# Windowed attention on one core: VectorE's passes over score tiles split by bank, four shared banks, and TensorE's order as strings

## The chip, the cores and the metric

The kernel runs on one core of a Trainium2 chip. The metric is device time in microseconds for one execution; lower is better. The engines of the core run in parallel and meet at semaphores: TensorE (matmuls, called PE in the profile), ScalarE (ACT), VectorE (DVE), GpSimd (POOL) and SyncE (SP, which here only issues DMAs). Matmul results land in PSUM, eight banks of 512 float32 columns on 128 partitions. Each engine takes its own instructions strictly in the order in which the program lists them.

## What is computed

Cross-shaped window attention on a 224 x 224 image with 96 channels. The first 48 channels attend within horizontal stripes of 8 rows, the other 48 within vertical stripes of 8 columns; each stripe has 1792 tokens. Cut to what matters:

```python
qkv = jnp.einsum('bhwc,cd->bhwd', x, wqkv)
q, k, v = qkv[..., :C], qkv[..., C:2*C], qkv[..., 2*C:]
# horizontal stripes, channels :C2, 28 windows of 8*W tokens
ah = softmax(einsum('bqc,bkc->bqk', qh, kh) * scale)
oh = einsum('bqk,bkc->bqc', ah, vh)
# vertical stripes, channels C2:, the same with windows of H*8 tokens
...
o = pad(oh) + pad(ov)
return jnp.einsum('bhwc,cd->bhwd', o, wo)
```

The shape that decides everything is the score matrix: 56 windows of 1792 x 1792 values, each of which needs an exponential.

## The kernel before, in words

**Tiles.** Windows are handled in pairs (28 pairs, index `P`; 0 to 13 horizontal, 14 to 27 vertical). For one pair, queries are cut into chunks `c` of 512, 512, 512 and 256 columns, keys into 14 blocks of 128. A score tile holds one key block against one query chunk for both windows of the pair: 128 x 1024, two PSUM banks, one bank for each window (for the last chunk two key blocks go together). A pair has 49 such tiles, 1372 in all.

**Two ways to the exponential.** A tile of kind A is scored by four matmuls into banks 0 and 1 or 2 and 3 (`qk_fn`, line 720), and ScalarE takes the exponential into one of 24 `PT` buffers (line 943). A tile of kind P or R is taken off ScalarE and goes through a polynomial on VectorE and GpSimd. TensorE scores it twice, through `s_fn` (line 733): once for the first pass and once more for the last. For kind P, VectorE makes `qb` from the low 16 bits of the scores ("p1", line 1224), GpSimd squares, adds and multiplies (lines 1151 to 1153), and VectorE adds the result onto the second scoring ("f", line 1248). For kind R, VectorE makes two passes over the first scoring (p1 and "p2", line 1237), GpSimd does one square (line 1150), then f follows. `KINDS` says which tiles of a pair are taken off, by chunk; `HOW[P][7]` picks one entry for each pair. Before, 20 pairs have 7 tiles off (all P), 7 pairs have 8 (seven P and one R), and the last pair has 5: 201 in all, 194 P and 7 R.

**Weighted sum and the rest.** `pv_fn` (line 746) multiplies a finished tile by V and adds into one bank for the chunk; VectorE copies the sum out ("ot", line 1206). Other small work fills in ("fills"): transposes of x (505), K, Q and V (522, 569) and the final projection (605, 641), each with a chain of evictions on VectorE (511, 527, 538, 576, 612 and 620, 648 and 653). DMAs of inputs and outputs are issued on SP's queue where a chain of VectorE ends.

**Banks.** Banks 0 to 3 belong to kind A. Banks 4 to 7 are the ring. Before, the chunk's sum takes bank 4 or 5, fills take any free bank of the ring, and the P and R tiles always take 6 and 7 (`PB0 = 6`, keys `PBK`), so that one such tile occupies the two until VectorE has read all 1024 columns.

**Order.** The program is made once, in Python. A planner (`step_pe`, `step_dve`, `step_pool`) steps a modelled time with durations from lines 30 to 36 and decides what each engine does next, by the thresholds in `HOW`. `Sched.commit` records each instruction with the semaphore values that it has to wait for, from `Sched.deps`. Buffers are known to it by keys: ("bank", 6), ("q", 2) for a `qb` buffer, ("PT", 5) for a `PT` buffer. Where an instruction touches a key that another one wrote, it waits for that one; only TensorE's dependences on itself are left out:

```python
for k in reads:
    for (s, _), v in self.wr.get(k, {}).items():
        if not (s == eng and eng == "pe"):
            d.add((s, v))
```

After that, `MERGE` gives the final order of kinds of work on TensorE and VectorE as strings ("q" score, "v" weighted sum, "p" a P or R tile, "f" and "o" fills, "s" a warm-up matmul), and `Sched.merge` reorders the lists accordingly.

Of the kernel before, what the change touches and what calls it, by code (L numbers as in the profile page):

```python
# [20 lines left out]

KINDS = ["PP PP PP ", "PPP PP PP ", "PPP PPP PP ", "PP PP P ", "PPR PP PP ", "PPR PR PP ", "PPR PPR PP ", "PPP PPR PP ", "PPR PPR PR ",
         "RPP RP PP ", "RPP RPP PP ", "PPP PRP PP ", "PPR PP PR ", "PPP PPP  ", "PPR PPP  ", "PPP PP  ", "PPP P  ",
         "PPPP PPP  ", "PPPP PP  ", "PPPP PPPR  "]
# [11 lines left out]
D_P1, D_SQ, D_AF, D_ML = 1.135, 1.9, 1.03, 2.08  # L36


HWIN, HLOW, COLD = 3.4, 0.56, 8.0
# [4 lines left out]

HOW = [
# [7 lines left out]
]  # L55

MERGE = {
    "pe": [
        "ssssssssssssssffffffffffsfsssqqqsfqsffqsfqpqfqpqfqpfqvvvfqqfvvvvqpfvqqpqfvqpqfvqpqfvqpqfvqpqfvqvfqffvqvvqopqvvvqvvqpfqvvqffqqfvqpf",
        "qvvqpvqvvqvvqpoqvvvqpqvfvqvvqpoqvvqvpqvvoqvvqpvqvfqvpqovqvvqpvoqvvqpvqvvfqpvqfqfqfpqvvqfqvvqpvqvvqpvqvoqfvfqvfqvvqpfqvvqvvqvfqvfqo",  # L60
        "oqvvqfvqpvqfqvpqvvqfvqpvqvfqpvqfvvqpfqvoqvvqpvqvvqvpqfvqvvqpoqvvqvpqvvvqfqpvqvvoqpvqfqvpqfqvvqvpoqvvqvvqffqvvqvfqpvqfvvqvpqfqvfqvo",
        "qfoqvvqvfqvpqfvqvpqvfqvvqpvqvvqfpqvvqvvqfvqpvqvfqpoqvvvqvpqfqvvqfqoovqfqvpqfvqvpqvfqvvvqpvqvfqvvqopqvvqvpqvfvqvpqfqfvqvfqfqfvqvpqv",
        "fqvvqvpqovqvvqpvqvvqvfqpvqvvqopqvvoqvvqpvqvfqvpqfqvpqvvoqvvqpvqfqpvqvvqvpoqvvqvvqpvqfqpvqfqvvqvfoqvvqpvqfvqffqvvqfpqvvqvfqfqfoqvvq",
        "pvqvvqopvqvvqvpqfvqvvqvvqfpqvvqvfqvpqfvvqvfqpvqvoqvpqvvqfqvpoqvvqvvqvpqfqvvvqopqvvvqvpqfqvvqpoqvvvqpvqfvqvfqfvqfvqfpqvoqvoqfqfqvvq",
        "fpqvvqvpqvfqvpqfvqvvqvvqpfqvvqpvoqvvqvvqfpqvvqvopqvvqvvqpfqvvqpoqvvvqpvqfqvpqfqvvqfqvopqvvqvfqvfqfvqfvvqvfqpvqfvqfqffqvqpfqvvqpvoq",
        "vvqpvqfvqvvvqopqvvqvvqpvoqvvqpvqvfvqvpqfqvvqopqvvvvqfoqfqvfqpqvvfvqfqffvqvvvqpqfvqpvqvoqvpqvvqfvqfqfpqvvqvpqvqvfqvvqpvqvvfqpvqfvqp",
        "vqvoqvpqvfvqvvqvvqpvqvoqvvqpvqvvoqpvqvvqpvqfqpvqvoqfoqfqfqvvqfpqvvvqvfqffqvvqfpqvoqvvvqpqvfvqpvqvvqpvqvfqpvqfqvvqpfqvvqfvqpvoqvvqp",
        "vqvfqvfqfvqpoqvvqvvqpvvqvoqpvqvfqvvqpvqfqfqvoqvvvvqopqvvvqvpqvfqvfqvfqpvqvvqpvqvvfqvpqovqvvqpvqfqffqffqvpqfvqvvqvqpvqfvqvpoqvqvvpq",
        "vvqvoqvpqvvvqfqpvqvvfqpqvvvvqpoqvvqvvpqfqvpqvvqfqfoqvoqvfvqvfqpvqfvqvpqfvqvvqopqvvqvfqpvqvfqfvqfqpvqfvqvvvqpfqvvqpvqvoqvvvqpoqvvvq",
        "pvqvfqvvqfpqvvvqopqvvqvvqpfqvvqfqpvqfqpvqfqvvfqooqvvqfvqvvfqpqvvvqfpqvfqvvqpvqvoqvpqvfvqvpqfqvvqpvqvvvqpvqfqvvqvpqvvqfvvqopqvvqvvv",  # L70
        "qopqvvvqffqvoqvvqpvqvvfqvvqopqvvvqpvqfvvqpvqfqpvqvvqopqvvvqvpqfqvoqvfqvqvfqpvqfvqfvqfpqvfqvvqfqfvqfoqvvvqpoqvvvqpvqfvqpqvvqfvvqpqv",
        "vvqfvqovqpvqfvqvpqfvqpqfvqvpqfvvqpqvvfqvqvvfqpvqovqvvqpoqvvvqpvqfqvvqpvqovqffqfqvpqfvqpqfvqvpqvvqpqfvqvpqvfvqvpqovqvvvqpoqvvvqvpqv",
        "vqvvqpoqvvqvvqvopqvvqvpqvfqvpqvfqvvqfvqvpqfvqvvqopqvvqfvqpvqvfqvpqfvqvpqfqvpqfvqvpqvfqvvqfpqvoqvvqvpqvvqvpqvoqvpqvvqvvqfvpqvoqvvqp",
        "vqvvqvpqvfqvvoqvqpqvvqvvqofqfvqovqvqpvqvqvfqpvqfqvfqvpqfqvqpfqvvqpvqvfqpvqvfvqpvqfvqvpqvvqovqvpqvoqvvvqpvqvvqfvqpvqvvqpvoqvvqvvqvo",
        "qvqpvqvoqvpqvvoqvvqpvqvfqpqvfvqpqsfqvvqpvvqvqvvfqvpqfvqvfqpqfvqvpqfqvpqfvqvvqpvqfvqvpqvvqovqvpqvvoqvpqvvqfqvvqfpqvvoqvpqvvqvvqfqpv",
        "qfqpoqvvqvpqvvqvqopqvvqvpqvvoqvvqpqvvvqpvqvfqpvqvfqpvqvvqfqvfqffqvvqfvqpfqvvqfvqpvqvqopvqvvqvoqvpqvvqvvqpvqvvqopqvvvqvpqvqvfvqpvqo",
        "vqpqvvqvvqvfqpvqfvqpqvvqopqvvvqvvqpfqvqofvqfqfvqvvqpvqvvqvfqfqpoqvvvqvpqvqvoqpvqvvqvvqpvqfqpfqvvqpfqvvqoqvpqvvqvvfqpoqvvqvvqpvqfvq",
        "vpoqvqvpqvvqvqvvqpqfvqpqvvqfpqvvoqvvqpvqvvqpqvfqpfqvvvqfqffvqoqvvpqvvvqfqvpqvvoqvpqvvqvvqpfqvvqfvqvpqvvoqvoqfvqvvoqvvqpqvfqvpqvfqv",
        "pqvfqvpqvqovqpvqvvvqvfqpvqvfqpvqvfqvfqfqpvqvvqvvfqpqfvqvpqvvqfqpvfqvvqpoqvvqvpqvvvqvqvvoqpvqvvvqpvqvqvfvqvpqvfqvvqpvqfvqpvqfvqpfqv",
        "fqvpqvvqvpqfvqpqvfqoqovqvvqfvqvvqopvqvvqvpqvvqfvqpoqvvqpvqvfqvpqvvqovqvpqvvqoqpvqvqvvqpvoqvvqpqoqvvqvpqvvfqvvqovqvvqpvqovqvvqpvqfv",  # L80
        "qvpqfqvpqfvqvvfqvqpqfqpvqfvqffqfqvpqfvqvvqpfqvvvqpoqvvqpvqvvqovqpvqvvqvvqfpqvoqvvvqpvqvvqoqvvqpvqvqpvoqvvqvvqpvoqvvqpvqvvqvvqvvqfv",
        "qvfqpvqfvqpvqvfqpfqvqpfqvvqpvqvfqooqvvqfvvqqpvfqpqfvqpqvvqvpqvfqvvqpvqvfqvpqvvvqvooqqfvqvvvqoqvpqvvqovqpvqvfvqpvqfvqvpqvvqfvqpvqvv",
        "qpfqvvqpvqvfqvpqfqvpqvvqfqpoqvvqvvqpoqvvqvvqvpqfqvpqvvqfvqvfqvfoqvvqpvqvvqvfqvvqopvqvqvvqovqpvqfvqvpqvvoqvvqpqvvqvpqvfqvpqvfvqvpqf",
        "qfvqvpqfvqvpqvvqfqpoqvvqvvqpvqvvqofqfvqvvqfpqvqvpqvvqfpqvvoqvvqovqvvqvvqfvqpvqvfqpqfvqpvqfvqvopqvvqvvqpvqfqpoqvvvqvvqpfqvvqfqvvqpf",
        "qvvqpvqvvqffqvpqfvqvvqovqvpqvoqvpqvvqvpqvvqfvqpqovqvpqvvqvvvqoqvpqvvqvpqvvqvopqvvqvvqvvqosvqooqvvqvoqvvqvpoqvvqvpqvvqvvqvvvqvvqvvq",
        "voooqvvvqvoqvvvqqooooqsqvvvvvvvoossssss",
    ],
    "dve": [
        "cccccccccccccccccfffffffffffpfpfpfffpffpfpfpfpfpftfffopopffffpfptpoopfpootpoopftpoopoopfpfffpftppooffffpftfoooofpfpfpfpftfppootpfp",
        "oopfpoopftpfopfoffpftfpfoofoofpfpfptpffptfpoopffoooofpfpftpfpoopffpfffftpfpoopfptoopoopftpfpoopfpopotpfpffoopffffptfffoopopopftfpf",  # L90
# [11 lines left out]
    ],  # L102
}
MRG, LATE, BLATE = 0.01, 0.1, 0.05


def kind_of(eng, tag):

# [3 lines left out]
    if eng == "dve":  # L112
        return {"p1": "p", "p2": "p", "f": "p", "ot": "t"}.get(k, "c" if not tag else "o" if tag[2] == "fin" else "f")
# [1235 lines left out]
```

## Time and profile before

| what | us |
|---|---|
| median of 3 runs (1097.43, 1095.25, 1097.43) | 1097.43 |
| span of the profiled execution, first to last instruction (its own device time is not listed apart from the runs) | 1094.3 |
| ScalarE's exponentials: first start 9.37, end of the last 1089.23 | 1171 of them |
| TensorE busy / VectorE busy / GpSimd busy | 1046.6 / 926.5 / 995.2 |
| TensorE's granted clock, mean share | 0.999 |

A busy time is the time in which at least one instruction of the engine was under way. The rows of the profile name a line of the code, an engine, an operation, what it writes and reads, its shape and how often it ran; behind the bar stand the busy time of the group, the mean duration of one in nanoseconds, and the time that the engine had been idle just before, with what ended that wait. Successive instructions of VectorE can overlap: the next may start before the one ahead has ended.

### The profile page before, as it was taken

The numbers are of one execution on the slowest core, as the hardware profiler recorded it, in microseconds if no ns is written. First come the engines' busy times: TensorE is split into PE (matmuls) and PEld (weight loads), VectorE is DVE, ScalarE is ACT, GpSimd is POOL, SyncE is SP. The second block draws the span as 40 slices with busy tenths as digits, with TensorE's granted clock in tenths as the row PEclk, the third lists the DMA queues.
The fourth block names the chain that finished last, engine by engine and source line by source line (L and its number), as shares of the span: only waits on it lengthen the run. The fifth ranks groups of instructions, "written<-read, shape, count | busy, mean of one in ns | idle before, by whom it ended". The sixth has DMA issues, their size and how long they took to land. (4 is left out here: it accounts for less than half of the span.)

```text
span 1094.3 us, 35438 instructions
## 1 busy us (share of the span) xinstructions
PE 1046.6 (96%) x14848; PEld 425.3 (39%) x14848; DVE 926.5 (85%) x1699; ACT 1082.6 (99%) x1182; POOL 995.2 (91%) x626
## 2 busy tenths in 40 slices
PE   8999999999999999999999999999999999999997
PEld 4334344444434444444333333333433333333333
DVE  6888788788888888888988989889888988888985
ACT  7999999999999999999999999999999999999998
POOL 6999899989989999997999999999899997999992
PEclk9999999999999999999999999999999999999999
DMA  4230231222123302302010120121110211211111
GB/s 86 47 52 15 40 52 20 39 47 39 30 38 52 53 9 46 53 2 52 27 28 15 41 50 16 44 47 21 43 43 12 60 40 22 48 41 43 25 22 34
DMA packets 183799, 40.91 MB, mean 37 GB/s; under 512 B 180408, under 2 KB 180952, under 8 KB 183640
## 3 DMA queue, kind: packets, MB, share of 16 engines
q1 hardware_dynamic: 182808, 38.22, 18.2%
q8 instruction: 116, 1.90, 0.7%
q10 hardware_dynamic: 832, 0.44, 0.1%
q14 instruction: 43, 0.35, 0.1%
HBM read 19.36 MB, written 19.27 MB: 35 GB/s over the span
## 5 line engine op out<-in xcount | busy, mean ns | idle before, releaser
L943 ACT ACTIVATE PT<-ps 128x1024 bf16<-128x1024 f32 x1171 | 1078.1, 1084 | 2.7 <-PE ps L720 1.7
L720 PE MATMUL ps<-QT_sb,KT_sb 49*64 49x512 bf16 (+1 forms) x5512 | 482.7, 365 | 40.3 <-ACT PT L943 24.4
L746 PE MATMUL ps<-PT,V_sb 128*49 128x512 bf16 (+1 forms) x3136 | 438.6, 360 | 0.5 <-DVE OT_sb L1206 0.2
L1153 POOL TENSOR_TENSOR PT<-PT,qb 128x1024 f16<-128x1024 f16 x194 | 412.4, 2126 | 16.2
L1151 POOL TENSOR_TENSOR PT<-qb 128x1024 f16<-128x1024 f16 x194 | 367.2, 1893 | 42.5 <-DVE qb L1224 22.3
L1248 DVE SCALAR_TENSOR_TENSOR PT<-ps,PT 128x1024 uint16<-128x1024 f32 x201 | 245.7, 1223 | 54.0 <-PE ps L733 35.0
L720 PEld LDWEIGHTS ps<-QT_sb,KT_sb 49*64 49x64 bf16 x5512 | 139.6, 103 | 384.7 <-ACT PT L943 367.7
L1224 DVE TENSOR_SCALAR qb<-ps 128x1024 f16<-128x1024 int16 x201 | 245.6, 1222 | 36.0 <-PE ps L733 32.7
L1152 POOL TENSOR_SCALAR PT<-PT 128x1024 f16<-128x1024 f16 x194 | 202.7, 1045 | 17.0
L746 PEld LDWEIGHTS ps<-PT,V_sb 128*49 128x49 bf16 x3136 | 131.7, 103 | 160.7 <-issue 121.3
L733 PE MATMUL ps<-QT_sb,KT_sb 50*64 50x512 bf16 (+2 forms) x1608 | 157.5, 381 | 1.5 <-DVE qb L1224 0.8
L653 DVE SCALAR_TENSOR_TENSOR out_all<-ps,rc,Ph_sb 128x96 bf16<-128x96 f32 x392 | 96.3, 311 | 2.6
L1206 DVE CAST OT_sb<-ps 113x512 bf16<-113x512 f32 x112 | 69.6, 622 | 20.1 <-PE ps L746 18.5
L538 DVE CAST QT_sb<-ps 128x512 bf16<-128x512 f32 (+1 forms) x111 | 68.5, 617 | 16.8 <-PE ps L522 16.1
L527 DVE TENSOR_SCALAR_CACHE_REDUCE KT_sb<-ps 128x512 bf16<-128x512 f32 x108 | 65.7, 618 | 3.8 <-PE ps L522 3.5
L576 DVE CAST V_sb<-ps 128x480 bf16<-128x480 f32 (+1 forms) x84 | 51.2, 620 | 5.1 <-PE ps L569 4.4
L620 DVE TENSOR_TENSOR Ph_sb<-ps,rc 128x480 bf16<-128x480 f32 (+1 forms) x84 | 52.2, 622 | 2.2
L733 PEld LDWEIGHTS ps<-QT_sb,KT_sb 50*64 50x64 bf16 (+2 forms) x1608 | 46.3, 105 | 18.8 <-DVE qb L1224 4.9
L522 PE MATMUL ps<-xT_sb,wq_sb 97*64 97x512 bf16 x224 | 41.9, 370 | 0.0
L522 PE MATMUL ps<-xT_sb,w_sb 97*64 97x512 bf16 x224 | 39.6, 365 | 0.0
L569 PEld LDWEIGHTS ps<-w_sb,xT_sb 96*64 96x64 bf16 x1568 | 32.8, 112 | 16.4 <-issue 10.0
L569 PE MATMUL ps<-w_sb,xT_sb 96*64 96x48 bf16 x1568 | 39.0, 191 | 0.0
(65 smaller groups left out, 352.9 us busy)
## 6 DMA issues: line engine op xcount, KB each, us to landing
xT_sb<-xt_dram SPq DMA_DIRECT2D x28, 336.0 KB, 4.0
out_dram<-out_all SPq DMA_DIRECT2D x388, 24.0 KB, 1.9
out_all<-in_x_dram SPq DMA_DIRECT2D x52, 168.0 KB, 2.7
xt_dram<-xT_sb SPq DMA_DIRECT2D x26, 336.0 KB, 5.9
xt_dram<-xT_sb SPq DMA_DIRECT2D x4, 168.0 KB, 4.4
Ph_sb<-in_x_dram SPq DMA_DIRECT2D x2, 168.0 KB, 3.6
Ph_sb<-in_x_dram ACTq DMA_DIRECT2D x2, 168.0 KB, 3.9
out_dram<-out_all ACTq DMA_DIRECT2D x4, 24.0 KB, 1.9
```

What stands on the lines that cost most here:

```text
L522: ins = e.matmul(bk[64 * w:64 * w + 64, 0:qs], lhsT=lw, rhs=xT_sb[b][:, w, q0:q0 + qs], start=True, stop=True)
L569: ins = e.matmul(bk[64 * h:64 * h + 64, j * C2:(j + 1) * C2], lhsT=xT_sb[b][0:C, w, t0:t0 + 64], rhs=w_sb[0:C, wblk(P, "v"), 0:C2], start= ...
L653: return e.scalar_tensor_tensor(out_sb[b][:, w, kt, :], bk3[:, s, 0:C], rc[ri][:, s:s + 1], Ph_sb[:, kt, j, :], ALU.mult, ALU.add)
L720: ins = e.matmul(bank(SETS[s] + w)[64 * kh:64 * kh + 64, i * t["qs"]:(i + 1) * t["qs"]], lhsT=KT_sb[b][64 * w:64 * w + CA, kt * 128 + 64 * ...
L733: ins = e.matmul(bank(PB0 + w)[64 * kh:64 * kh + 64, 0:512], lhsT=KT_sb[b][64 * w:64 * w + nr, kt * 128 + 64 * kh:kt * 128 + 64 * kh + 64] ...
L746: ins = e.matmul(bank(pb)[64 * w:64 * w + CA, 0:t["qs"]], lhsT=V_sb[b][:, w, kt, :], rhs=PT[slot][:, ca:ca + t["qs"]], start=st and i == 0 ...
L943: S.commit("act", 0.0, D_ACT, None, lambda e, s=s, slot=slot: e.activation(PT[slot][:], ps[:, 512 * SETS[s]:512 * SETS[s] + 1024], ACTF.Ex ...
L1151: sq = lambda e: e.tensor_tensor(y, q, q, ALU.mult)
L1152: af = lambda e: e.tensor_scalar(y, y, PB, 128.0 * PA, ALU.add, ALU.mult)
L1153: ml = lambda e: e.tensor_tensor(y, y, q, ALU.mult)
L1224: S.commit("dve", t, D_P1, D_P1 + SEMD + (0.12 if tl["kind"] == "R" else 0.0), lambda e: e.tensor_scalar(qb[tl["qb"]][:], low16(), m, a, A ...
L1248: S.commit("dve", t, D_P1, D_P1 + SEMD, lambda e: e.scalar_tensor_tensor(PT[tl["slot"]][:].bitcast(U16), ps[:, PB0 * 512:(PB0 + 2) * 512], ...
```

## The change

Five things change together.

1. `KINDS` has one entry, "PPR PPR PP", for every pair: two P and one R in the first and second chunk, two P in the third. That is 8 of 49 tiles, 168 P and 56 R in all.
2. VectorE's passes p1, p2 and f are issued for each half of a tile, one bank of 512 columns each (`emit_p`), and a bank is given back as soon as its half is through.
3. The P and R tiles may take any two of the four ring banks (`get_banks`), and so may fills and the chunk's sum take any one.
4. TensorE's order is written out as 28 strings (`ORDER`): q score tile, 1 and 2 first and second scoring of a P or R tile, v weighted sum, k preparing fill, f final fill. The planner's decisions for TensorE, `HOW`, `MERGE`, and the warm-up matmuls during the run go; the order on VectorE and GpSimd follows from a model of the two (`dve_step`, `pool_step`), in which a half pass takes `D_H = 0.6`.
5. The memset of V's column of ones stands earlier in GpSimd's lead.

`Sched.deps`, the buffers (24 `PT`, 5 `qb`), the fills, their chains and the DMAs are as before. Cut to its core:

```diff
-KINDS = ["PP PP PP ", "PPP PP PP ", "PPP PPP PP ", "PP PP P ", "PPR PP PP ", "PPR PR PP ", "PPR PPR PP ", "PPP PPR PP ", "PPR PPR PR ",
...
+KINDS = ["PPR PPR PP "]
...
-D_P1, D_SQ, D_AF, D_ML = 1.135, 1.9, 1.03, 2.08
+D_H, D_SQ, D_AF, D_ML = 0.6, 1.9, 1.03, 2.08
...
+ORDER = [
...
+    "1qfvvqq1vvqfqvvqfvqv1qvvqvqvvq1vqkkvqkvq1q2qvq2q1qkvqvvvq2vqvvq1qvkfqvvqv2qkqvkvq2qkvvq1qvkvq2qvvkvq1qvvkvqvqvvvkq2fqvvvq",
...
-        PB0 = 6
-
-        def low16():
-            return ps[:, PB0 * 512:(PB0 + 2) * 512].bitcast(I16).rearrange("p (n t) -> p n t", t=2)[:, :, 0]
+
+        def low16(bi):
+            return bank(bi).bitcast(I16).rearrange("p (n t) -> p n t", t=2)[:, :, 0]
...
+        for i in range(2):
+            pool_now(["vones"], lambda e, i=i: e.memset(V_sb[i][:, :, :, C2:CA], 1.0), 0.2)
...
-                        ins = e.matmul(bank(PB0 + w)[64 * kh:64 * kh + 64, 0:512],
+                        ins = e.matmul(bank(bp[w])[64 * kh:64 * kh + 64, 0:512],
...
+        def emit_p(what, tl, h):
+            bi, cols = tl["bp"][h], slice(512 * h, 512 * h + 512)
+            q, y = qb[tl["qb"]][:, cols], PT[tl["slot"]][:, cols]
+            bk, qk, ptk = [("bank", bi)], [("q", tl["qb"])], pt_keys(tl["slot"])
+            if what == "p1":
+                m, a = (HS * 2.0 ** -16, HS * RB) if tl["kind"] == "R" else (2.0 ** -16, 0.5 + PK)
+                fn, reads, writes = lambda e: e.tensor_scalar(q, low16(bi), m, a, ALU.mult, ALU.add), bk, qk
+            elif what == "p2":
+                fn, reads, writes = lambda e: e.scalar_tensor_tensor(
+                    y.bitcast(FP16), low16(bi), -RA * 2.0 ** 16, q, ALU.add, ALU.mult), bk + qk, ptk
             else:
...
+                fn, reads, writes = lambda e: e.scalar_tensor_tensor(
+                    y.bitcast(U16), bank(bi), 128.0, y.bitcast(FP16), ALU.mult, ALU.add), bk + ptk, ptk
+            S.commit("dve", 0.0, D_H, D_H + SEMD, fn, reads, writes, fresh=writes if h == 0 and what != "f" else [])
...
+        def dve_step():
+            t = dve_next()
+            best = None
+            for i, d in enumerate(dq):
+                if d["ready"] <= t + 0.02:
+                    key = {"ot": -1e6, "p2": -9e5 + d["ready"], "p1": 1e5 + d["ready"], "f": 1e5 + d["ready"]}.get(d["what"], d["ready"])
...
+        def get_banks(n):
+            while True:
+                free = sorted((bi for bi in RING if bi not in busy), key=lambda bi: bank_free[bi])
+                if len(free) >= n:
+                    busy.update(free[:n])
+                    return free[:n], bank_free[free[n - 1]]
+                one_step()
...
+        def do_s(c):
...
+            tl["bp"], t = get_banks(2)
+            st = pe_start("A", max(r, t))
+            tm["pe"] = st + D_MM
+            seen = st + L_PV + (0.05 if c == "2" else 0.0)
+            emit_s(tl, c)
+            rd = max(seen, qb_t[tl["qb"]]) if c == "1" else max(seen, tl["mid_t"], slot_t[tl["slot"]])
+            for h in range(2):
+                dq.append(dict(what="p1" if c == "1" else "f", ready=rd + h * 1e-4, dur=D_H, tl=tl, h=h))
...
+        for c in "".join(ORDER):
+            if c == "q":
+                do_q()
+            elif c in "12":
+                do_s(c)
+            elif c == "v":
+                do_v()
+            else:
+                do_fill(c)
+            at[0] += 1
+            advance(tm["pe"] + 0.2)
```

More of the change, by code (lines that the diff above doesn't have):

```diff
@@ L123, in __init__ @@
         self.log = []
-        self.kinds = {k: [] for k in self.cnt}
         self.wr = {}
@@ L188, in fresh @@
         self.rd.pop(k, None)
-    def share(self, t):
-        while self.stream and self.stream[0][0] + self.stream[0][1] < t - HWIN:
-            self.stream.pop(0)
-        return sum(min(t, s + d) - max(t - HWIN, s) for s, d in self.stream) / HWIN
     def commit(self, eng, start, dur, lat, fn, reads, writes, fresh=(), tag=""):
@@ new lines, in emit_pv, with emit_s, emit_ot @@
+        def emit_pv(tl, first, last, pb):
+            S.commit("pe", 0.0, D_MM, L_PV, pv_fn(tl, tl["slot"], first, last, pb), pt_keys(tl["slot"]) + v_keys(tl["P"] % 2),
+                     [("bank", pb)], fresh=[("bank", pb)] if first else [])
+        def emit_s(tl, c):
+            keys = [("bank", bi) for bi in tl["bp"]]
+            S.commit("pe", 0.0, D_MM, L_PV, s_fn(tl, 50 if c == "1" else 53 if tl["kind"] == "R" else 52), kt_keys(tl), keys, fresh=keys)
+        def emit_ot(P, c, pb):
+            q0, qs = CH_Q0[c], CH_SIZES[c]
+            S.commit("dve", 0.0, 0.6, 0.75, lambda e: e.tensor_copy(OT_sb[P % 2][0:64 + CA, q0:q0 + qs], bank(pb)[0:64 + CA, 0:qs]),
+                     [("bank", pb)], [("OT", P % 2, c)])
@@ new lines, in pool_step @@
+        def pool_step():
+            t = pool_next()
+            best = None
+            for i, tl in enumerate(pq):
+                if tl["mid_t"] <= t + 0.02 and (best is None or tl["no"] < pq[best]["no"]):
+                    best = i
+            tl = pq[best]
+            m = tl["mid"].pop(0)
+            st = max(t, tl["mid_t"])
+            tm["pool"] = st + m[1]
+            tl["mid_t"] = st + m[1] + SEMP
+            S.commit("pool", 0.0, m[1], m[1] + SEMP, m[2], m[3], m[4])
+            if not tl["mid"]:
+                take_last(pq, best)
@@ L1272, in bass_standalone__window_attn_cswin__vision_kernel @@
[L1272 to L1282 removed]
+                tl["ready2"] = True
@@ new lines, in pe_start, with wait_for @@
+        def pe_start(m, ready):
+            t = tm["pe"]
+            if tm["mode"] != m:
+                t += (SW_AB if m == "B" else SW_BA) + (W_FIN if tm["mode"] == "A" and tm["fin"] else 0.0)
+                tm["mode"], tm["run"] = m, 0
+            else:
+                tm["run"] += 1
+                if tm["run"] == 1:
+                    t += W_PE
+            tm["fin"] = False
+            return max(t, ready)
+        def wait_for(ok):
+            while not ok():
+                one_step()
@@ new lines, in k_of, with do_q @@
+        def k_of(tl):
+            return [(tl["P"], c) for c in sorted({chunk_of_col(kt * 128) for kt in tl["kts"]})]
+        def do_q():
+            tl = act_seq[ia[0]]
+            P, c = tl["P"], tl["c"]
+            s = ia[0] % 2
+            ks = k_of(tl)
+            wait_for(lambda: all(k in k_t for k in ks) and (P, c) in q_t)
+            r = max([set_free[s] + MRG, q_t[P, c] + MRG] + [k_t[k] + MRG for k in ks])
+            st = pe_start("A", r)
+            tm["pe"] = st + D_MM
+            slot = slot_free.pop(0)
+            go = max(st + L_MM, tm["act"], slot_t[slot])
+            tm["act"] = go + D_ACT
+            tm["end"] = max(go + M_ACT, tm["end"] + P_ACT)
+            tl["ready"] = set_free[s] = tm["end"] + SEMA
+            tl["slot"] = slot
+            emit_qk(tl, s, slot)
+            cand.append(tl)
+            ia[0] += 1
+            if P not in begun:
+                begun.add(P)
+                if P + 1 < NP:
+                    x_t[P + 1] = 0.0 if ph_of(P + 1) == 0 else st + (10.5 if ph_of(P) == 0 else 5.0)
+                    queue_prep(P + 1)
+                fin_q.extend(f for _, f in fin_fills(P, 2 if P == NP - 1 else FS))
@@ new lines, in pick, with do_v @@
+        def pick():
+            own = [tl for tl in cand if (tl["P"], tl["c"]) == pv_chunks[pv_open[0]]]
+            return min(own, key=lambda tl: tl["ready"]) if own else None
+        def do_v():
+            P, c = pc = pv_chunks[pv_open[0]]
+            wait_for(pick)
+            wait_for(lambda: v_n.get(P, 0) == 3)
+            r = v_t[P]
+            if acc[0] is None:
+                b, t = get_banks(1)
+                acc[0] = b[0]
+                r = max(r, t)
+            tl = pick()
+            st = pe_start("B", max(tl["ready"], r))
+            tm["pe"] = st + D_MM
+            take_last(cand, cand.index(tl))
+            first = pv_left[pc] == pv_total[c]
+            pv_left[pc] -= 1
+            emit_pv(tl, first, pv_left[pc] == 0, acc[0])
+            slot_free.append(tl["slot"])
+            slot_t[tl["slot"]] = st + L_PV
+            n_done[P] += 1
+            if pv_left[pc] == 0:
+                dq.append(dict(what="ot", ready=st + L_PV, dur=0.07 + CH_SIZES[c] * 0.001026, pc=pc, bank=acc[0]))
+                acc[0] = None
+                pv_open[0] += 1
@@ new lines, in do_fill @@
+        def do_fill(c):
+            f = (prep_q if c == "k" else fin_q).pop(0)
+            g = f["gives"]
+            P, r = g[1], 0.0
+            if c == "f":
+                need = f["needs"][0][1:]
+                wait_for(lambda: need in ot_t)
+                r = ot_t[need]
+            else:
+                r = x_t[P]
+                if g[0] == "K":
+                    assert P < 2 or n_done[P - 2] == 49
+                    if P > 0 and ph_of(P) == 0:
+                        wait_for(lambda: t_n.get(P, 0) == 4)
+                        r = max(r, t_t[P])
+                elif g[0] == "QB":
+                    wait_for(lambda: all((P, z) in k_t for z in range(NCH)))
+                    r = max([r] + [k_t[P, z] for z in range(NCH)])
+                elif g[0] == "Q":
+                    wait_for(lambda: P in kb_t)
+                    r = max(r, kb_t[P])
+                elif g[0] == "V" and ph_of(P) == 0:
+                    r = max(r, t_t.get(P, 0.0))
+            b, t = get_banks(1)
+            d = f["pe_dur"]
+            st = pe_start(f["mode"], max(r, t))
+            tm["pe"] = st + d
+            tm["fin"] = f["mode"] == "A"
+            emit_fill(f, b[0])
+            dq.append(dict(what="fill", ready=st + d + L_FILL + (0.08 if c == "f" else 0.0), dur=f["chain"][0][0], fill=f, bank=b[0], stage=0))
```

635 lines of the change are left out of this document (166 added, 469 removed), and 7 rows, old and new, of the table HOW.

## The prediction

> **What bounds the kernel now.** I read the page's first table, then its groups by line, then who waited for whom, then VectorE's timeline, then busy time by stretch.
>
> ```profile
> PE 1046.6 (96%) x14848; PEld 425.3 (39%) x14848; DVE 926.5 (85%) x1699; ACT 1082.6 (99%) x1182; POOL 995.2 (91%) x626
> ...
> L943 ACT ACTIVATE PT<-ps 128x1024 bf16<-128x1024 f32 x1171 | 1078.1, 1084 | 2.7 <-PE ps L720 1.7
> L1153 POOL TENSOR_TENSOR PT<-PT,qb 128x1024 f16<-128x1024 f16 x194 | 412.4, 2126 | 16.2
> L1151 POOL TENSOR_TENSOR PT<-qb 128x1024 f16<-128x1024 f16 x194 | 367.2, 1893 | 42.5 <-DVE qb L1224 22.3
> L1248 DVE SCALAR_TENSOR_TENSOR PT<-ps,PT 128x1024 uint16<-128x1024 f32 x201 | 245.7, 1223 | 54.0 <-PE ps L733 35.0
> L1224 DVE TENSOR_SCALAR qb<-ps 128x1024 f16<-128x1024 int16 x201 | 245.6, 1222 | 36.0 <-PE ps L733 32.7
> L1152 POOL TENSOR_SCALAR PT<-PT 128x1024 f16<-128x1024 f16 x194 | 202.7, 1045 | 17.0
> ```
>
> ScalarE works 1078.1 us of the 1094.3 us span on 1171 exponentials (L943), one per 0.921, and stands idle 2.7 before them. It is the bound. TensorE's busy share means little by itself: its weight loads wait for ScalarE to free a score buffer.
>
> ```profile
> PEld ps L720 <- ACT PT L943: 367.7, 952, 0.9
> ```
>
> A tile taken off ScalarE is worth 0.92 us only if the engines that take it have room. So the next view is VectorE's timeline (start, duration):
>
> ```profile
> 519.67 0.69 DVE L538 CAST QT_sb<-ps 128x512 bf16<-128x512 f32 x1 [0.28 <-PE ps L522]
> 520.28 0.18 DVE L612 RECIPROCAL rc<-ps 128x5 f32<-128x5 f32 x1
> 520.50 0.66 DVE L620 TENSOR_TENSOR Ph_sb<-ps,rc 128x480 bf16<-128x480 f32 x1
> 521.19 1.22 DVE L1248 SCALAR_TENSOR_TENSOR PT<-ps,PT 128x1024 uint16<-128x1024 f32 x1
> 522.33 0.68 DVE L538 CAST QT_sb<-ps 128x512 bf16<-128x512 f32 x1
> ```
>
> Two distances are to be seen. An instruction followed by an independent one hands over before its own end: the 512-wide cast after 0.61 of its 0.69, the full pass after 1.14 of its 1.22. An instruction followed by one that needs its result does not: the reciprocal lasts 0.18 and L620, which reads it, starts after 0.22, so 0.04 behind the end instead of 0.08 ahead. A wait of VectorE on itself thus costs about 0.115 us, unless other work stands in between.
>
> And how full VectorE has been (columns: stretch, length, then busy us with counts for PE, PEld, DVE, ACT, POOL, then clock and DMA):
>
> ```profile
> 0.00:14.50 14.50, 12.31 (x137) 7.20 (x141) 7.56 (x33) 9.49 (x17) 7.25 (x37) 1.00 0.20 55
> 849.00:887.00 38.00, 35.09 (x448) 13.44 (x442) 35.51 (x76) 38.00 (x43) 36.88 (x22) 1.00 0.29 67
> 793.00:803.00 10.00, 9.16 (x110) 3.36 (x106) 9.85 (x25) 10.00 (x12) 9.74 (x6) 1.00 0.17 33
> 1085.00:1094.30 9.30, 4.86 (x91) 2.92 (x83) 4.44 (x20) 4.23 (x5) 0.00 (x0) 0.92 0.21 40
> ```
>
> Its fullest 38 us are 35.51/38.00 = 93%, its fullest 10 us 98.5%.
>
> **The change, part by part.**
>
> **ScalarE.** 28 pairs x 8 = 224 tiles off instead of 201: 23 exponentials fewer, 23 x 0.921 = 21.2 us. If nothing else gave way the span would be about 1073.
>
> **GpSimd.** A P tile costs 1.893 + 1.045 + 2.126 = 5.064, an R tile one 1.89 square (L1150, 7 of them, 13.3). Before 194 P and 7 R: 996. After 168 P and 56 R: 851 + 106 = 957. It gets lighter by 39 and is no bound. Costed at nothing.
>
> **TensorE.** In the written orders the letters change between the two kinds of work 2144 times before and 1819 times after. The 23 moved tiles each take two score groups (L733: 157.5/402 = 0.39) for one (0.41), at most 8.6 us more. What a change of kind costs no single row gives. Bounds: nothing, or 0.11 each (36 us), the mean of the two constants that the kernel itself keeps for it on line 30. Either way TensorE is not the later one, because it waits for a score buffer 367.7 us today. Costed at nothing; its cover is VectorE. Twelve warm-up matmuls fall away; the clock row reads 9 in every slice with TensorE 96% busy, so nothing there too, and at the tail under a microsecond. The memset of V's ones (L414, 0.51) moves ahead of some memsets and copies on GpSimd in the lead, all over before 11.3 us; the first user of V comes at 18.95. Nothing. DMAs are the same ones, issued in the same places of VectorE's chains from SP's queue.
>
> **VectorE.** Here the change puts its load, in three steps.
>
> (1) What it holds now. Busy is 926.5; it stopped 391 times for more than 50 ns (counted over the timeline) and each stop shows a tail of 0.08 that work right behind it would have covered: 31. 184 short gaps of 0.034 behind self-waits are held time: 6. So about 900 must be held. 409 full passes (201 + 201 + 7) at 1.14 are 466; the other work is 434.
>
> (2) The new passes: p1 and f for 224 tiles, p2 for 56, in halves: 2 x (224 + 224 + 56) = 1008 at 0.605 (the 512-wide cast's 0.61, and half of the way from 0.35 for 256 and 1.14 for 1024) = 610. Sum 1044. The cut itself costs 504 x 0.07 = 35 of this; 49 more p2 and 46 more p1 and f passes cost 95 x 1.14 = 108.
>
> [...]
>
> (3) The wait nobody wrote down. Both halves carry the same key (("q", i) or ("PT", slot)), and deps() drops a dependence on the own engine for TensorE only. So half 1 waits for half 0's semaphore, although they touch different columns, and p2 waits for p1. That is 504 junctions between halves and 56 from p1 to p2: 560 x 0.115 = 64 us if all are open, 0 if other work always stands between. Behind the waiting half, in order, stand all of VectorE's evictions, and behind those TensorE's next bank. Before, the two passes stood next to each other only 6 times in the order written out (one pair of banks); now both halves become ready at once, and with one bank for the sum and two for the tile only one is left for an eviction to come in between. I take half of them open: 32. Sum **1076**, bounds 1044 and 1108.
>
> Outside its loaded time VectorE idles 14.5 - 7.56 = 6.9 at the start and 9.3 - 4.4 = 4.9 at the end: 12. The free time in which this could hide is gone: ScalarE's new load from first exponential (9.4) to last is 1148 x 0.921 = 1057, less than 1076. **VectorE becomes the bound.** It also can't be full. Bounds for its share: 93% (best 38 us) and 98.5% (best 10 us). With two halves always queued it resembles the 10 us stretch more, so I take 97.5%. Span: 1076/0.975 + 12 = 1116. The median of the runs is 1097.4, 3.1 over the span; with that, **1119 us**, 2.0% slower.
>
> **The rivals.**
>
> *Self-waits cost nothing, or are covered (faster).* VectorE's load is then 1044: 1044/0.975 + 12 + 3 = 1086. For it: evictions and the parts of a final chain (reciprocal, then products) come ahead of passes when ready, so a half can fill their wait and they its; any two of four banks remove the 68 us that L1248 and L1224 wait for L733. Against it: the 0.04 behind the reciprocal. It decides below some 150 open junctions (17 us), at which 1061/0.98 + 15 = 1098 is break-even. Chance 0.24. [...]
>
> *TensorE's written order makes it worse.* The order is fixed for halves of 0.6 back to back. When a half takes 0.72, TensorE stands at the first bank not yet free, with exponentials' scores queued behind it, and VectorE then runs dry. Its share falls to the 93 to 94% of the best 38 us: 1076/0.935 + 15 = 1166. For: in-order queues, all four engines over 90%. Against: VectorE has been fuller for 10 us. Chance 0.17.
>
> *It cancels.* About 150 open junctions and 98%: 1098, no change within 0.2%, which is about what a measurement here can tell. Chance 0.07. It is also the case in which the free choice of banks does nothing beyond what the old alternation did.
>
> **How the numbers follow.** Forecast 0.52 (own range 1102 to 1140), worse 0.17, faster 0.24, equal 0.07. Low end: self-waits free and 98%, 1044/0.98 + 15 = 1080. High end: all junctions open, 1108/0.975 + 15 = 1151. Some 0.08 lies under and 0.12 over. Faster 0.24, same 0.07, slower 0.69.
>
> **What would show it.** Exponentials x1148, passes x448, x448 and x112 of 128x512 with rows near 0.69. VectorE's busy time of some 1080 or more, over ScalarE's. In its timeline, second halves that start 0.72 behind the first ones, not 0.61, where they are neighbours. ScalarE idle tens of us, waiting for L720's scores, and TensorE's waits for VectorE risen from a few us to tens. Wrong if ScalarE stays 99% busy, if neighbours start 0.61 apart, or if evictions stand between most halves.

## The result, and the profile after

| | median us | range | ratio to the kernel before, 95% interval |
|---|---|---|---|
| before | 1097.43 | 1095.25 to 1097.64 (4 runs) | |
| changed | 1122.72 | 1120.92 to 1126.92 (4 runs) | 1.0241 [1.0219, 1.0262] |

The change makes the kernel 2.4% slower, 26 us by the ratio, though ScalarE has 23 exponentials fewer, worth 21 us. Some 47 us went elsewhere. (Differences between kernels are worked out from the ratios below, 0.01 being 11 us, because not all kernels ran beside the same runs of the one before.) Medians are over all executions and ratios leave out the few in a slower state, so that a median can lie above what its ratio gives. The profiled execution spans 1119.0 us. These are the rows of its page that answer to those shown of before (lines have moved: L796 is the exponential, L834 p1, L836 p2, L839 f):

```profile
PE 1071.9 (96%) x14928; PEld 428.7 (38%) x14928; DVE 1071.6 (96%) x2298; ACT 1081.1 (97%) x1159; POOL 955.8 (85%) x597
...
L796 ACT ACTIVATE PT<-ps 128x1024 bf16<-128x1024 f32 x1148 | 1076.5, 1041 | 25.7 <-PE ps L635 16.6
...
L839 DVE SCALAR_TENSOR_TENSOR PT<-ps,PT 128x512 uint16<-128x512 f32 x448 | 305.7, 687 | 14.0 <-PE ps L648 4.9
L834 DVE TENSOR_SCALAR qb<-ps 128x512 f16<-128x512 int16 x448 | 305.6, 686 | 11.1 <-PE ps L648 4.9
...
L836 DVE SCALAR_TENSOR_TENSOR PT<-ps,qb 128x512 f16<-128x512 int16 x112 | 77.1, 689 | 4.2
```

The counts are those of the change (1148, 448, 448, 112). VectorE has gone from 926.5 us busy to 1071.6; ScalarE's idle before its exponentials from 2.7 to 25.7. GpSimd is lighter by 39.4, as summed. Next, VectorE's timeline of the changed kernel (start, duration; "x2" merges two instructions of the same line):

```profile
599.83 0.18 DVE L580 RECIPROCAL rc<-ps 128x5 f32<-128x5 f32 x1
599.95 0.69 DVE L834 TENSOR_SCALAR qb<-ps 128x512 f16<-128x512 int16 x1
600.55 1.21 DVE L585 SCALAR_TENSOR_TENSOR out_all<-ps,rc,Ph_sb 128x96 bf16<-128x96 f32 x5
...
611.99 1.41 DVE L834 TENSOR_SCALAR qb<-ps 128x512 f16<-128x512 int16 x2
613.31 2.73 DVE L839 SCALAR_TENSOR_TENSOR PT<-ps,PT 128x512 uint16<-128x512 f32 x4
```

At 599.95 a half pass has other work behind it, and that starts 0.60 later. At 611.99 the two halves of one tile are neighbours: together 1.41 for two rows of 0.69, so the second starts 0.72 behind the first. Counted over the whole timeline, 392 neighbours of one tile stand about 0.034 apart where others overlap by 0.08.

The waits of the changed kernel (who waited for whom, us in total, times, longest):

```profile
PEld ps L635 <- ACT PT L796: 199.9, 569, 0.8
...
PEld ps L648 <- DVE PT L839: 31.4, 93, 0.8
PEld ps L648 <- DVE qb L834: 25.8, 70, 0.9
ACT PT L796 <- PE ps L635: 16.6, 52, 1.0
```

TensorE's weight loads used to wait 368 us for ScalarE and, all rows of that kind together, 46 for VectorE; now it is 200 and 205. The wait has moved from the engine that was the bound to VectorE, and at 52 places ScalarE now waits for TensorE.

The page also follows the work back from the last instruction, at each step to what released it, and gives the share of the span that this chain spends on each engine. In the changed kernel:

```profile
DVE 46%; PE 40%; ACT 5%; issue 5%; POOL 3%; DMA 0%; DVEq 0%; ACTq 0%; POOLq 0%
```

The chain goes back and forth between VectorE and TensorE, and only 5% of it is ScalarE.

**A correction to what stands ahead.** The description of the kernel says that `MERGE` gives the final order. Nothing in the file calls `Sched.merge`; the planner's own order is what runs. So the two numbers that the prediction took from those strings are not of the program: counted over the traces, TensorE changes its kind of work 1672 times before and 1819 times after, 147 more and not 325 fewer, and two passes were neighbours on VectorE not once in 409.

### The profile page after: what moved, and what is told of

The parts are those of the page before. It is cut to its first block, busy times and chain, and to the rows that moved or that the text cites. A ratio compares the mean times of both kernels' runs of the same rounds, so it can differ in the third digit from the quotient of the medians.

```text
span 1119.0 us, 36142 instructions
## 1 busy us (share of the span) xinstructions
PE 1071.9 (96%) x14928; PEld 428.7 (38%) x14928; DVE 1071.6 (96%) x2298; ACT 1081.1 (97%) x1159; POOL 955.8 (85%) x597
## 4 chain that ended last, share of the span: by engine, by line
DVE 46%; PE 40%; ACT 5%; issue 5%; POOL 3%; DMA 0%; DVEq 0%; ACTq 0%; POOLq 0%
PE ps L661 15%; DVE qb L834 14%; PE ps L635 13%; DVE PT L839 12%; PE ps L648 5%; ACT PT L796 5%; DVE out_all L585 5%; DVE PT L836 4%; PE ps L454 3%; DVE OT_sb L813 2%; DVE KT_sb L459 2%; DVE xT_sb L443 2%; PE ps L501 2%; PE ps L537 1%; DVE V_sb L508 1%
## 5 line engine op out<-in xcount | busy, mean ns | idle before, releaser
L796 ACT ACTIVATE PT<-ps 128x1024 bf16<-128x1024 f32 x1148 | 1076.5, 1041 | 25.7 <-PE ps L635 16.6
L661 PE MATMUL ps<-PT,V_sb 128*49 128x512 bf16 (+1 forms) x3136 | 455.2, 362 | 1.5 <-DVE PT L839 0.4
L846 POOL TENSOR_TENSOR PT<-qb 128x1024 f16<-128x1024 f16 x168 | 316.7, 1893 | 107.8 <-DVE qb L834 70.1
L850 POOL TENSOR_TENSOR PT<-PT,qb 128x1024 f16<-128x1024 f16 x168 | 355.5, 2124 | 9.1
L839 DVE SCALAR_TENSOR_TENSOR PT<-ps,PT 128x512 uint16<-128x512 f32 x448 | 305.7, 687 | 14.0 <-PE ps L648 4.9
L834 DVE TENSOR_SCALAR qb<-ps 128x512 f16<-128x512 int16 x448 | 305.6, 686 | 11.1 <-PE ps L648 4.9
L635 PEld LDWEIGHTS ps<-QT_sb,KT_sb 49*64 49x64 bf16 x5420 | 147.6, 104 | 256.8 <-ACT PT L796 199.9
L648 PE MATMUL ps<-QT_sb,KT_sb 50*64 50x512 bf16 (+2 forms) x1792 | 181.6, 395 | 18.2 <-DVE qb L834 3.9
L849 POOL TENSOR_SCALAR PT<-PT 128x1024 f16<-128x1024 f16 x168 | 175.3, 1043 | 14.3
L848 POOL TENSOR_TENSOR PT<-PT 128x1024 f16<-128x1024 f16 x56 | 106.0, 1893 | 15.4 <-DVE PT L836 11.2
L585 DVE SCALAR_TENSOR_TENSOR out_all<-ps,rc,Ph_sb 128x96 bf16<-128x96 f32 x392 | 97.5, 306 | 0.6
L836 DVE SCALAR_TENSOR_TENSOR PT<-ps,qb 128x512 f16<-128x512 int16 x112 | 77.1, 689 | 4.2
```

The source lines that it names most:

```text
L585: return e.scalar_tensor_tensor(out_sb[b][:, w, kt, :], bk3[:, s, 0:C], rc[ri][:, s:s + 1], Ph_sb[:, kt, j, :], ALU.mult, ALU.add)
L635: ins = e.matmul(bank(SETS[s] + w)[64 * kh:64 * kh + 64, i * t["qs"]:(i + 1) * t["qs"]], lhsT=KT_sb[b][64 * w:64 * w + CA, kt * 128 + 64 * ...
L648: ins = e.matmul(bank(bp[w])[64 * kh:64 * kh + 64, 0:512], lhsT=KT_sb[b][64 * w:64 * w + nr, kt * 128 + 64 * kh:kt * 128 + 64 * kh + 64], ...
L661: ins = e.matmul(bank(pb)[64 * w:64 * w + CA, 0:t["qs"]], lhsT=V_sb[b][:, w, kt, :], rhs=PT[slot][:, ca:ca + t["qs"]], start=st and i == 0 ...
L796: S.commit("act", 0.0, D_ACT, None, lambda e, s=s, slot=slot: e.activation(PT[slot][:], ps[:, 512 * SETS[s]:512 * SETS[s] + 1024], ACTF.Ex ...
L834: fn, reads, writes = lambda e: e.tensor_scalar(q, low16(bi), m, a, ALU.mult, ALU.add), bk, qk
```

## The experiments

All on the chip, each timed beside the kernel before (medians 1095.5 to 1098.1 there).

**Self-waits gone: a key for each half.**

```diff
-            return [("PT", slot)]
+            return [("PT", slot, h) for h in range(2)]
...
-            bk, qk, ptk = [("bank", bi)], [("q", tl["qb"])], pt_keys(tl["slot"])
+            bk, qk, ptk = [("bank", bi)], q_keys(tl["qb"])[h:h + 1], pt_keys(tl["slot"])[h:h + 1]
...
-            qk, yk = [("q", tl["qb"]), "pser"], pt_keys(tl["slot"])
+            qk, yk = q_keys(tl["qb"]) + ["pser"], pt_keys(tl["slot"])
```

> Each half of a qb or PT buffer gets its own key, so a half pass no longer waits for the other half; order, tiles and banks stay those of the changed kernel. Theory (VectorE is the bound, and its waits on itself make it so): the changed kernel's trace has 392 neighbours of one tile with 0.034 us between them instead of an overlap of 0.08; 392 x 0.115 = 45 us of VectorE go, its load falls to about 1040, under ScalarE's 1057, and the time to 1080 to 1095 us; ScalarE's idle before its exponentials falls from 25.7 us to under 10. Rival A (TensorE's written order, with 1819 changes of kind against 1672 in the trace of before, is the bound): 1110 to 1123 us. Rival B (a semaphore wait is free): 1120 us, and neighbours still 0.72 apart.

Measured: 1100.12 us, ratio 1.0049 [1.0021, 1.0076]; 1.9% or 21 us better than the changed kernel and still 0.5% slower than before. First the page's row of the engines, then VectorE's timeline, the waits of this kernel (L837 is p1, L842 f) and its chain:

```profile
PE 1061.8 (97%) x14928; PEld 428.6 (39%) x14928; DVE 1044.9 (95%) x2298; ACT 1071.6 (98%) x1159; POOL 956.0 (87%) x597
```

```profile
600.60 1.28 DVE L837 TENSOR_SCALAR qb<-ps 128x512 f16<-128x512 int16 x2
601.80 2.55 DVE L842 SCALAR_TENSOR_TENSOR PT<-ps,PT 128x512 uint16<-128x512 f32 x4
```

```profile
PEld ps L635 <- ACT PT L799: 256.2, 714, 0.8
...
PEld ps L648 <- DVE PT L842: 21.4, 68, 0.7
```

The chain that ended last, in this kernel (as far as the page could follow it):

```profile
PE 52%; ACT 18%; DVE 8%; issue 5%; POOL 2%; DMA 0%; ACTq 0%; DVEq 0%; SPq 0%; POOLq 0%
```

The same pair takes 1.28 for 1.41, four halves 2.55 for 2.73. Nothing but waits was taken away, so the self-waits cost 21 us of the 47: shown. TensorE's waits for VectorE, all rows together, fell from 205 to 143 us, and VectorE's part of the chain from 46% to 8%. The time lies just above the range of the theory, and ScalarE's idle fell to 14.4, not under 10; rivals A and B fall as causes of those 21, but something else holds the remaining 26 us over what ScalarE's share would allow.

**Other work put between.** The model that orders VectorE's work learns of the self-wait; the waits stay.

```diff
                 emit_p(what, tl, h)
+                for z in dq:
+                    if z.get("tl") is tl and z["h"] > h and z["what"] == what:
+                        z["ready"] = max(z["ready"], st + d["dur"] + 0.12)
```

> The model that orders VectorE's work is told that a half starts at the earliest 0.12 us behind the end of the other half of its tile, so other work that is ready is put between; keys, tiles and TensorE's strings stay. The waits remain in the program. Theory (open junctions are what costs): the 392 open ones fall to 150 to 300 and the time to 1100 to 1115 us. Rival (nothing is ready to come between, or what comes between is late for somebody else): 1115 to 1130 us.

Measured: 1122.82 us, ratio 1.0249 [1.0226, 1.0273], the same as the changed kernel. Open neighbours fell only from 392 to 320. The theory's count was missed: in the model's time there was mostly nothing else ready to put between. The 72 that did close, 8 us at 0.115 each, brought nothing that can be told. The time lies in the range of the rival.

**The cut undone: whole passes over two neighbouring banks.**

```diff
+            return ps[:, bp[0] * 512:(bp[0] + 2) * 512].rearrange("p (b n) -> p b n", b=2)
...
+                if n == 2:
+                    two_of = [(bi, bi + 1) for bi in free if bi + 1 in free]
+                    free = min(two_of, key=lambda z: max(bank_free[bi] for bi in z)) if two_of else ()
```

> One pass over a tile as before (128x1024, 1.14 us), over two neighbouring banks of the four (4-5, 5-6 or 6-7); tiles and TensorE's strings stay those of the change. It undoes the cut alone. Theory: VectorE's load is 434 + 504 x 1.14 = 1009 us, 67 less than in the changed kernel, so ScalarE is the bound again: 1075 to 1095 us. Rival (TensorE's order, searched for banks that come free one by one, stalls where two come free at once): 1100 us or more with VectorE under 93% busy and TensorE waiting for it.

Measured: 1233.43 us, ratio 1.1263 [1.1203, 1.1324]. The theory is far off, the rival right in kind: VectorE is 84% busy and ScalarE idles 117 us before its exponentials. Two things were undone at once, so the next run separates them. (TensorE's granted clock was 0.975 in the profiled execution; the fastest of the four took 1227.40 us at 0.983, the slowest 1244.31 us at 0.960, so part of the time goes with the clock.)

**Neighbouring banks with halves.** The kernel with a key for each half, and the restriction of banks:

```diff
+                if n == 2:
+                    two_of = [(bi, bi + 1) for bi in free if bi + 1 in free]
+                    free = min(two_of, key=lambda z: max(bank_free[bi] for bi in z)) if two_of else ()
+                    free = sorted(free, key=lambda bi: bank_free[bi])
```

> The kernel with keys by half (1100 us), passes cut in halves as in the change, but a P or R tile may only take two neighbouring banks of the four. It tells the cut from the choice of banks, which the kernel with whole passes (1233 us) undid together. Theory (the choice of any two banks carries most of it, since the sum's bank often leaves two free ones that are not neighbours): 1160 us or more. Rival (the cut carries it): 1100 to 1130 us.

Measured: 1242.04 us, ratio 1.1231 [1.1135, 1.1328]. Its engines, and ScalarE's wait:

```profile
PE 1114.5 (90%) x14928; PEld 433.0 (35%) x14928; DVE 1058.6 (85%) x2298; ACT 1102.0 (89%) x1159; POOL 958.0 (77%) x597
...
L799 ACT ACTIVATE PT<-ps 128x1024 bf16<-128x1024 f32 x1148 | 1097.4, 1032 | 125.3 <-PE ps L635 112.3
```

With these strings the free choice of banks carries 130 us (1.0049 to 1.1231). Part of this goes with the clock, which was 0.947 in the profiled execution (1240.79 us) and 0.962 in the fastest one (1223.35 us): 126 us of the profiled one ran at half clock, which by estimate from that stretch alone loses at most half of it, 63 us. With neighbours only, halves (1.1231) do as whole passes do (1.1263), so a bank that comes back half a pass sooner is worth nothing that can be told there. In this program the cut goes together with the choice of any two banks; whether one whole pass could have read two banks that are not neighbours was not tried.

**The tile count alone,** in the kernel before:

```diff
-                off = KINDS[HOW[P][7]][c]
+                off = KINDS[6][c]
```

> The kernel before with 8 of 49 tiles off ScalarE in every pair (two P and one R, two P and one R, two P), its own planner, whole passes, banks 6 and 7. The tile count alone. Theory: VectorE's load is 900 + 95 x 1.14 = 1008 us, 92% of the span, more than in any of its pairs so far (at most 90%); ScalarE's exponentials take 1057; 1078 to 1092 us if the planner can feed them. Rival (two fixed banks, held 1.14 us for each pass, can't carry 504 passes: one tile after the other needs score 0.4, hand-over and pass, some 1.9 us each, 504 x 1.9 = 958 plus stalls): 1095 us or more, with VectorE waiting for L733 more than the 68 us of before.

Measured: 1312.52 us, ratio 1.1985 [1.1951, 1.2019]. The theory fails by 220 us. The rival's range and its stated sign hold: VectorE waits for L733 143 us rather than 68. Its cause, the two fixed banks, is not shown by that: ScalarE idles 212 us, 184 of it for scores (L720), and the planner's thresholds, set for the tiles of the kernel before, may be as much at fault. The two were not tried apart. TensorE's granted clock was 0.902 in the profiled execution, and the single times go with it, from 1311.07 us at 0.902 to 1318.84 us at 0.894; how much of the 220 us is the clock's was not measured. Room on VectorE (79% busy) was not enough for the planner to use it.

**VectorE lighter by 52 us, without and with self-waits.**

```diff
+            if what == "f" and tl["kind"] == "R":
+                fn = lambda e: e.scalar_tensor_tensor(
+                    y[:, 0:64].bitcast(U16), bank(bi)[:, 0:64], 128.0, y[:, 0:64].bitcast(FP16), ALU.mult, ALU.add)
```

> The kernel with keys by half (1100 us), and the last pass of the 56 R tiles covers 64 of 512 columns of each half, so 448 of 512 columns of those tiles keep GpSimd's square: 112 passes lose 448 x 1.04 ns = 0.466 us, 52 us of VectorE in all. Theory (with the self-waits gone VectorE is still what sets the pace, at 95%): 1075 to 1090 us, ScalarE's floor being about 1075. Rival (TensorE's order, which is the same, sets it now): 1094 to 1102 us.

> The changed kernel (1122.7 us) with its self-waits, and the last pass of the 56 R tiles covers 64 of 512 columns of each half: 52 us of VectorE less, about what the self-waits cost it (45), taken from elsewhere. Theory (what the self-waits cost is VectorE's load, whatever it is made of): 1095 to 1108 us. Rival (each self-wait makes its own tile late, and load elsewhere does not matter): 1115 to 1123 us.

Measured: without self-waits 1099.12 us, ratio 1.0032 [1.0012, 1.0052], against 1.0049 [1.0021, 1.0076]: nothing that can be told. With them 1117.55 us, ratio 1.0203 [1.0157, 1.0249], against 1.0241 [1.0219, 1.0262]: 4 us, within the intervals. The engines of the two, in this order:

```profile
PE 1059.4 (97%) x14928; PEld 427.0 (39%) x14928; DVE 1000.6 (91%) x2298; ACT 1071.0 (98%) x1159; POOL 956.4 (87%) x597
```

```profile
PE 1072.0 (96%) x14928; PEld 427.9 (38%) x14928; DVE 1029.2 (92%) x2298; ACT 1079.7 (97%) x1159; POOL 957.0 (86%) x597
```

Both theories fall. VectorE lost 42 to 44 us of busy time and the time hardly moved: what it lost came back as idle time, in the kernel with self-waits 54.6 us of waiting for TensorE instead of 17.9. The same amount taken out as self-waits was worth 21. The lighter passes took 18 us off TensorE's waits for VectorE (205 to 187), the removed self-waits 62 (205 to 143). So it is not the sum on VectorE that sets the end. That it is when VectorE hands back each tile fits these waits, but no run changed the hand-over alone. One doubt stays: this cut lightens 2 of 8 tiles of a pair, and stretches with P tiles alone keep their load.

**GpSimd for VectorE: fewer R tiles.**

```diff
-KINDS = ["PPR PPR PP "]
+KINDS = ["PPR PPR PP ", "PPP PPR PP "]
...
+KIND_OF = [0, 1] * 14
```

> The kernel with keys by half (1100 us), and every other pair has seven P and one R for six P and two R. VectorE loses 14 x 2 x 0.605 = 17 us, GpSimd gains 14 x (5.06 - 1.89) = 44 us, to 1000 us. TensorE's strings stay. Theory (VectorE sets the pace and GpSimd has room): 1088 to 1097 us. Rival (the strings ask for the second scoring of a tile when an R would be ready, and a P is ready 3.2 us later): 1100 to 1125 us.

Measured: 1162.09 us, ratio 1.0608 [1.0581, 1.0636], beyond both. ScalarE, TensorE and VectorE have waits of up to 6 us here; in the kernel with a key for each half the first two rows are at most 1.1 us at a time:

```profile
ACT PT L799 <- PE ps L635: 65.0, 84, 6.0
PEld ps L648 <- DVE PT L842: 39.0, 69, 6.1
...
DVE PT L842 <- POOL PT L853: 26.5, 13, 6.1
```

VectorE was lighter here too. The strings fit one mix of tiles; a tile that is ready 3 us later than its letter (GpSimd's rows of a P tile sum to 5.06 us, that of an R tile is 1.89) stops TensorE, and ScalarE behind it. The clock fell too, to 0.951 in the profiled execution (1165.58 us); the fastest took 1158.31 us at 0.960, so part of the time goes with it.

**TensorE lighter.** ScalarE's score matmuls cover three quarters of the columns; the rest of the bank keeps older scores.

```diff
+                n = t["qs"] if t["no"] <= 8 else t["qs"] * 3 // 4
...
-                                           rhs=QT_sb[b][64 * w:64 * w + CA, t["q0"]:t["q0"] + t["qs"]], start=True, stop=True)
+                                           rhs=QT_sb[b][64 * w:64 * w + CA, t["q0"]:t["q0"] + n], start=True, stop=True)
```

> The kernel with keys by half (1100 us), and the score matmuls of ScalarE's tiles cover three quarters of the columns; the rest of the bank keeps older scores, of which ScalarE takes the exponentials as usual. 1148 x 4 matmuls lose a quarter of some 0.054 us each, 62 us of TensorE. Theory (VectorE still sets the pace): 1092 to 1102 us. Rival (TensorE does): 1075 to 1088 us.

> The changed kernel (1122.7 us) with the same cut of ScalarE's score matmuls to three quarters of the columns, 62 us of TensorE. Theory (VectorE sets the pace): 1112 to 1123 us. Rival (TensorE's order and its 147 more changes of kind set it): 1100 us or less.

Measured: 1106.14 us, ratio 1.0070 [1.0038, 1.0103], and 1133.96 us, ratio 1.0327 [1.0285, 1.0369]. The first can't be told from the kernel without the cut (1.0049 [1.0021, 1.0076]), the second is slower (1.0241). As medians they say nothing of TensorE's load, because its clock fell, to 0.959 in the profiled execution of the first and 0.967 in that of the second. The second one in two stretches (columns as in the prediction; the clock is the number behind the busy times):

```profile
930.00:955.00 25.00, 23.88 (x254) 8.68 (x254) 20.11 (x37) 20.02 (x22) 18.82 (x12) 0.66 0.03 7
900.00:925.00 25.00, 23.39 (x374) 10.55 (x374) 24.77 (x70) 24.01 (x26) 18.77 (x12) 1.00 0.24 55
```

At a clock of 0.66 the same 25 us hold 254 matmuls instead of 374. Inconclusive as a test. Single executions at like clock give a hint: of the kernels with a key for each half, the one with shorter score matmuls took 1094.39 us at 0.987, the one without 1106.27 us at 0.987.

**TensorE heavier.** Every eighth score tile of ScalarE's is scored twice, in the kernel with a key for each half and in the one before.

```diff
-            ... qk_fn(tl, s, 2 if 1 <= ia[0] <= NTWICE else 1) ...
+            ... qk_fn(tl, s, 2 if 1 <= ia[0] <= NTWICE or ia[0] % 8 == 0 else 1) ...
```

> The kernel with keys by half (1100 us, where a lighter VectorE gave nothing), and every eighth score tile of ScalarE's is scored twice with the same result: 143 x 0.22 = 31 us more for TensorE, in places spread evenly; its clock has no reason to fall. Theory (with the self-waits gone, TensorE's in-order list sets the pace): 1122 to 1135 us. Rival (latencies between engines do, and TensorE has room): 1100 to 1108 us.

> The kernel before with the same: every eighth score tile scored twice, 146 x 0.22 = 32 us more for TensorE; its planner is not told. Theory (before, ScalarE sets the pace and TensorE's 368 us of waiting for it can take this in): 1096 to 1105 us. Rival (TensorE has no room here either): 1115 us or more.

Measured: 1120.39 us, ratio 1.0214 [1.0194, 1.0235], so 18 us more for 31; and 1115.03 us, ratio 1.0164 [1.0146, 1.0181], so 18 us more for 32. The clock stayed at 0.999 in both profiles. The first lies between theory and rival, the second at the edge of its rival. Somewhat over half of the added work comes through in both (0.58 and 0.56). The 31 and 32 are estimates, from 0.22 us for a second scoring: in the trace of before the early tiles that are scored twice take 0.63 for their eight matmuls, the others 0.41 for four; TensorE's busy time by the profile rose by 21.8 and 25.7. TensorE's list has little room in either kernel, although its weight loads waited 256 and 368 us for ScalarE. These waits fell to 230 and 337, by nearly the work that was added, and the time rose all the same. A reading that fits, not shown: the waits lie at single letters, and time lost at one of them is made up only in part at the next.

## Why the prediction was right, and where its steps failed

The time (1122.7 for 1119) and the sign were right, and so was the mechanism that made most of the slowdown: with the self-waits out, 0.5% of the 2.4% was left. Its steps did not all hold.

**The wait nobody wrote down (step 3) held.** Halves share a key, so a half waits for the other; the price of 0.115 us read from the reciprocal is what the trace shows (0.72 behind 0.60). The term was mis-sized: half of 560 were taken as open, 392 were, 45 us for 32. Taking the waits out gave back 21 us. The rival without self-waits was priced at 1086 us; without them the kernel took 1100, 14 us that the sum does not have.

**VectorE's load was right by number, in part by luck.** Busy 1071.6 and 16.5 of short gaps behind self-waits, less 117 exposed tails of 0.08, make 1079 for the predicted 1076; over the 1107 us outside lead and tail this is 97.5%, the share that was taken. Two errors cancelled: the self-waits came 13 us higher than taken, and the load without them, 1079 - 45 = 1034, 10 lower than the predicted 1044. The half pass itself was right, 0.60 to 0.61 for 0.605, though "half of the way" from 0.35 to 1.14 would be 0.75; 512 columns lie a third of the way from 256 to 1024. One stated sign was missed: VectorE's busy time was to be 1080 or more and over ScalarE's, and it is 1071.6 against 1081.1.

**"VectorE becomes the bound" failed as it was worked out, from its load.** If the load set the end, 52 us less of it would have given tens of us; they gave 4 and 2. What the traces show in its place: TensorE's list is in order (the trace of the changed kernel has the 1819 changes of kind of its strings), and it stands until VectorE hands back banks (205 us of such waits for 46, 100 of them ahead of the scorings of P and R tiles), and the chain that ended last is shared, 46% on VectorE and 40% on TensorE. The reading that fits is that a late hand-over holds everything listed behind, ScalarE's scores among it, so that lateness at every tile costs while load taken from a few tiles is worth next to nothing; it is argued from these waits, not shown by a run of its own. Nearly the right total came from dividing by a share that was itself estimated, and that agreement does not prove the step.

**"TensorE costed at nothing" failed.** It rested on strings that no code uses; in fact there are 147 more changes of kind. Its other ground, that TensorE waits 368 us for a score buffer, does not hold either: in the kernel before, 32 us of added scoring cost 18. With self-waits gone the kernel stays 26 us above what 23 exponentials fewer would give, and added TensorE work comes through by over half. That its list holds these 26 us is likely (without self-waits 52% of the chain is TensorE, 8% VectorE) but not shown: no run took work from TensorE at an unchanged clock, and the changes of kind were not tried alone. The missing warm-up matmuls were costed at nothing too: the changed kernel has one stretch of 6.8 us at half clock near 930 us, by estimate at most half of it, 3.4 us, lost, and the one before has none between its lead and its tail (1.00 from 14.5 to 1085 us). That is the fastest of the changed kernel's executions, 1120.92 us at a mean clock of 0.995; the other three had 0.993 to 0.986, the last with 1126.92 us, so the clock took somewhat more there. No run put the warm-up matmuls back.

**The rivals.** "Self-waits cost nothing" fell with the first experiment. The one on TensorE's written order named the wait that the trace shows, TensorE standing at banks not yet free; but VectorE did not run dry as it said (97.5%, not 93 to 94%), and the price was far under its 1166. That the free choice of banks does little, which the rival of no change implied, is refuted for these strings by 130 us.

The errors point to the likeliest next step, which was not tried: keys for each half together with strings searched anew for the measured durations.

## What to carry to other kernels

When an instruction is split, split the keys by which its dependences are tracked as well; otherwise the parts wait for each other, and in the trace this shows as a start a little behind the neighbour's end where others overlap (here 0.034 us behind where others overlap by 0.08, worth 21 us). Before trusting a table in a program, look for the call that uses it, and count orders in the trace. On engines with in-order lists near full load, ask also when a result is handed back, and not only how busy an engine is: test it by lightening the engine without touching the waits (here 42 to 44 us less of VectorE's busy time brought 2 to 4).

## What the runs showed of the hardware that was not expected

TensorE's granted clock fell to half for longer when its work got lighter, without long pauses: in the changed kernel with shorter score matmuls seven stretches, 71.6 us in all, ran at half clock (0.967 as the mean of its span), and the longest gap between matmuls there, lead and tail apart, was 0.83 us. In the changed kernel itself the longest was 0.82 us, and one stretch of 6.8 us ran at half clock. In the kernel before the longest was 0.54 us and the clock never fell there (1.00 from 14.5 to 1085 us). TensorE was 94% busy by the profile in the stretch at full clock shown above (23.39 of 25 us) and 96% in the one at a mean of 0.66 (23.88 of 25 us). What sets it off, no run here shows.

A semaphore wait of VectorE on its own instruction just ahead cost 0.12 us in these traces, also between instructions that share no data: 0.72 for 0.60. Taking the waits out was worth 21 us.
